# A windowed attention and token-mixing kernel in one written-out order of tasks: another order, other engines and homes for the small steps

## The chip, the cores and the metric

The kernel runs on one core of one Trainium2 chip. The metric is the device time of one execution in microseconds. The kernel before takes 250.66 us (median of three runs: 250.23, 250.66, 251.75).

## The reference

For four batches of eight heads, 768 positions and head width 64, the reference does attention in which a query sees the first four keys (sinks) and the 128 keys up to itself. The heads side by side are the rows x of a block with 512 columns. The block mixes positions and then columns:

```python
scores = np.where(is_sink | in_window, scale * (q @ k.T), -1e9)
x = softmax(scores) @ v                      # heads side by side: [4, 768, 512]
a1 = alpha1 * x + beta1
tok = np.einsum('ts,bsd->btd', w_tok, a1)    # w_tok 768 x 768
u = x + lam * tok
a2 = alpha2 * u + beta2
ch = np.maximum(a2 @ w_ch1, 0.0) @ w_ch2     # 512 -> 2048 -> 512
return u + lam * ch
```

All inputs and the output are float32 in device memory.

## The kernel before

**A list of tasks.** The kernel first builds a list of 1230 tasks, numbered in the order in which the program's loops create them. A task is one to a few dozen instructions on one engine: a load, a cast, the six transposes of one tile, the scores of one tile, one group of matmuls, one relu. Each knows the tasks it needs and the buffers it uses. Then `Plan.emit` writes the tasks out, and four tables written into the source say how:

- `ORDER` is the sequence of task numbers. Every engine executes its own instructions in this order, and never passes one that waits.
- `ENGINES` has one digit for each task: 0 is ScalarE (ACT), 1 VectorE (DVE), 2 TensorE (PE), 3 GpSimd (POOL), 4 SyncE (SP). SP only issues DMAs; ACT issues some as well and POOL issues those of w1, which are cast on the way.
- `HOMES` has one hexadecimal digit for each buffer, in the order in which tasks first use it. A buffer of a kind (say "nat") lives in one of the kind's homes (say 8), and must wait until every reader of the buffer that was there before has finished. A load into an occupied home so waits on the engine's queue that issues it, and every load behind it in that queue waits as well.
- `IDLES` puts warm-up matmuls of no use ahead of five tasks, to keep PE going at the start (67 ahead of task 46, 25 ahead of task 90).

The kinds that matter here are "nat" (8 homes, a pair of heads of q or k in float32, all 768 positions), "vnat" (4, a tile of v), "wst" (4, two 128-row blocks of w_ch2 in float32, at the start also three tiles of v), "d" (4 banks of PSUM) and "E", "x", "xh", "u16", "hT" for what lies between.

**The stages.** Batch 0 is handled first. Loads of q, k and v (tasks 6 to 25; `load_qk`, L413, `load_v0`, L441), the transposes of q and k on PE with their evacuation into qkT (`trans`, L505: cast, six transposes on L532 or L535, then the evacuation through the helper `copy`, L168 on ACT or L170 on the others), scores (L640 to L709), exponentials on ACT (L667, L714), masks (L682 on DVE, L607 on POOL), the product with v (L739, L746) with normalisation (L771, L772), halves of the scaled x (xh, L781 on POOL or DVE) and the token mix (`tok`, L868, matmuls on L880). w_tok is loaded in six tiles, scaled on ACT (L842) or DVE (L844) and transposed by PE (wT, L837). Casts of v (vfs) go through `cast_v0` (tasks 63 to 67).

Then each batch b goes through the two column matmuls while the next batch's attention is interleaved: PE alternates groups of four matmuls of h (`mlp1`, L952, matmuls L960; relu on ACT L966 or DVE L968) and of ch (`mlp2`, L1260, L1269) with the attention tasks of batch b+1. Batches 1 to 3 replace part of the two column matmuls by seven products of sums (`prod`, L1163, L1199; sums of the weights `w1S` on L993 and `w2s` on L1114), batch 3 in pairs (`mlp1_pair`, L1021, L1041). At the end the adds on L1212 and stores on L1218 write the last output.

**Loads around the change.** w_ch1 comes in four chunks of which POOL issues the requests (`load_w1`, L474, L476: tasks 32 to 35). A small DMA on SP (`gate`, L481, L483) lets SP wait for a chunk's landing before it goes on: task 36 holds the eight q and k loads of batch 1 (170 to 177; `load_qk`, L425) and those of w_ch2 (`load_w`, L469, L472) until chunk 1 has landed. w_ch2's blocks are multiplied into f16 as w2f (`cast_w2`, L854, L859; tasks 181 to 202) in pairs from one "wst" buffer. The casts of batch 1's q and k tiles are tasks 363, 366, 369, 372, 375, 378, 381 and 384, the transposes that follow each one are the numbers one higher.

Of the kernel before, what the change touches and what calls it, by code (L numbers as in the profile page):

```python
# [80 lines left out]
def kernel(  # L81
# [129 lines left out]
    for r in range(NR):  # L211
# [18 lines left out]
        6, 7, 0, 26, 1, 10, 5, 2, 9, 11, 45, 18, 8, 19, 48, 3, 22, 15, 46, 4, 49, 12,  # L230
        50, 14, 17, 47, 13, 16, 90, 43, 103, 39, 41, 91, 28, 72, 104, 95, 53, 54, 63,
        51, 42, 73, 52, 21, 44, 74, 20, 96, 109, 100, 40, 107, 110, 65, 24, 68, 108, 92,
        69, 55, 61, 56, 93, 97, 101, 98, 59, 30, 94, 102, 111, 23, 99, 62, 113, 57, 114,
        25, 112, 116, 60, 105, 115, 58, 27, 128, 64, 106, 117, 31, 131, 135, 29, 129,
        125, 132, 138, 66, 130, 179, 78, 126, 122, 178, 140, 118, 139, 123, 197, 127,
        136, 119, 137, 32, 70, 146, 120, 141, 133, 33, 84, 79, 134, 124, 144, 147, 80,
        85, 71, 150, 121, 86, 142, 75, 67, 154, 143, 151, 76, 148, 158, 155, 145, 152,
        77, 87, 166, 156, 159, 81, 162, 167, 160, 88, 163, 82, 168, 89, 213, 157, 164,
        34, 35, 83, 209, 153, 217, 149, 214, 218, 210, 229, 219, 211, 215, 212, 226,
        165, 216, 36, 230, 185, 220, 161, 177, 223, 222, 176, 232, 221, 224, 204, 225,  # L240
        175, 227, 257, 169, 237, 233, 279, 238, 199, 234, 171, 258, 273, 280, 231, 186,
        259, 228, 274, 182, 277, 172, 260, 241, 278, 174, 246, 200, 295, 170, 248, 247,
        291, 296, 37, 181, 187, 243, 293, 292, 242, 289, 198, 294, 384, 267, 188, 290,
        281, 268, 173, 271, 349, 282, 180, 285, 272, 358, 301, 351, 286, 378, 303, 189,
        203, 297, 302, 192, 304, 249, 366, 190, 379, 298, 250, 287, 369, 380, 385, 205,
        288, 283, 191, 375, 386, 367, 265, 284, 368, 352, 370, 363, 376, 266, 253, 381,
        377, 371, 299, 254, 372, 615, 364, 206, 300, 382, 201, 365, 373, 275, 374, 383,
        357, 261, 276, 183, 387, 408, 262, 614, 263, 409, 202, 269, 184, 411, 410, 395,
        264, 239, 621, 617, 412, 397, 240, 270, 388, 400, 396, 235, 616, 196, 244, 398,
        401, 255, 245, 236, 390, 256, 193, 359, 389, 251, 399, 207, 311, 195, 252, 391,  # L250
        424, 426, 393, 335, 392, 360, 425, 636, 312, 194, 427, 208, 336, 394, 648, 428,
        413, 634, 419, 414, 622, 404, 420, 337, 405, 429, 402, 415, 313, 422, 416, 421,
        361, 441, 305, 403, 442, 638, 423, 626, 406, 314, 640, 619, 437, 315, 430, 443,
        316, 435, 431, 641, 338, 436, 362, 618, 433, 306, 438, 649, 341, 317, 432, 407,
        444, 637, 644, 307, 345, 439, 339, 620, 318, 445, 434, 628, 635, 450, 642, 308,
        451, 340, 440, 452, 639, 446, 453, 417, 319, 447, 645, 323, 418, 320, 309, 448,
        643, 658, 321, 324, 623, 449, 322, 329, 625, 659, 454, 646, 325, 347, 647, 330,
        455, 343, 326, 344, 353, 355, 464, 456, 465, 348, 466, 460, 650, 457, 467, 327,
        458, 331, 629, 461, 459, 462, 653, 632, 651, 463, 656, 332, 654, 356, 472, 627,
        652, 333, 342, 310, 38, 655, 660, 624, 480, 473, 468, 469, 470, 474, 885, 665,  # L260
        471, 476, 481, 475, 482, 488, 477, 350, 483, 492, 489, 478, 630, 490, 657, 493,
        479, 514, 491, 516, 328, 515, 882, 663, 518, 880, 517, 879, 498, 666, 661, 664,
        502, 499, 354, 508, 519, 512, 346, 509, 662, 678, 513, 671, 484, 679, 676, 486,
        503, 504, 487, 485, 677, 506, 877, 672, 680, 548, 507, 526, 505, 549, 334, 674,
        631, 522, 527, 907, 546, 681, 523, 633, 903, 528, 547, 534, 878, 529, 890, 675,
# [12 lines left out]
        986, 773, 752, 913, 886, 761, 919, 774, 604, 767, 918, 598, 762, 763, 768, 777,
        764, 779, 920, 923, 780, 987, 988, 989, 990, 914, 991, 992, 993, 755, 915, 778,
        608, 756, 926, 930, 735, 609, 924, 927, 931, 925, 753, 736, 781, 737, 893, 928,  # L280
        775, 782, 738, 892, 929, 934, 754, 932, 769, 610, 935, 941, 770, 819, 776, 894,
        942, 939, 820, 821, 940, 937, 936, 823, 749, 822, 748, 945, 824, 938, 747, 827,
        933, 948, 950, 750, 943, 952, 951, 825, 953, 787, 828, 944, 807, 788, 797, 826,
        808, 949, 946, 829, 954, 798, 801, 830, 791, 802, 947, 956, 792, 783, 957, 994,
        995, 996, 997, 961, 789, 784, 962, 958, 963, 964, 955, 790, 785, 959, 811, 965,
        805, 812, 786, 795, 806, 960, 967, 796, 799, 793, 968, 970, 966, 972, 794, 813,
        969, 971, 815, 973, 814, 809, 800, 974, 816, 803, 810, 976, 804, 978, 837, 975,
        979, 977, 835, 838, 980, 841, 836, 818, 839, 843, 842, 840, 981, 845, 844, 998,
        846, 817, 1002, 832, 831, 1006, 999, 1003, 1000, 1014, 1007, 1004, 1001, 833,
# [1193 lines left out]
```

## Time and profile before

| | before |
|---|---|
| median of three runs | 250.66 us |
| span of the profiled execution | 248.4 us |
| the profiled execution's own time beside its span | not listed apart; the runs' median is 2.26 us above the span |
| PE busy | 242.9 us (98%) |
| DVE busy | 208.0 us (84%) |
| ACT busy | 136.1 us (55%) |
| POOL busy | 126.0 us (51%) |
| moved by DMA | 38.80 MB |

The profile is one execution. Its page lists the busy time of each engine, 40 slices of the span with the share of each engine and of the DMA engines in tenths, the chain of work that ended last, and the groups of instructions by source line. Other views are the timeline of one engine (start and duration in us, engine, line, operation, output and input, and in brackets the engine's idle time before it with what released it), the busy time by windows, and the answers for one tile or one line (durations in ns as min/median/max, with the first and last start). SPq, POOLq and ACTq are the queues that issue DMAs; what such a row shows as its duration is the issue, not the transfer.

### The profile page before, as it was taken

To read this page: it belongs to the slowest core of one execution; us is meant where nothing else is said; L and a number is where in the kernel's file an instruction comes from. 1 tells how busy PE (TensorE), PEld (TensorE's weight loads), DVE (VectorE), ACT (ScalarE), POOL (GpSimd) and SP (SyncE) were. 2 spreads that over 40 slices of the span, in tenths; PEclk is the share of its full clock that TensorE was granted. 3 is DMA by queue.
4 is the path that set the end of the run, shared out by engine and by line. 5 is a ranking of instruction groups with operands and counts; after the bars stand their busy time and mean duration, and the time that the engine had idled before them with its cause. 6 is when DMAs were issued, how large, how long until landed. Compare 5 with 4: busy or idle time off the path is not lost.

```text
span 248.4 us, 5583 instructions
## 1 busy us (share of the span) xinstructions
PE 242.9 (98%) x2151; PEld 159.2 (64%) x2151; DVE 208.0 (84%) x437; ACT 136.1 (55%) x229; POOL 126.0 (51%) x139
## 2 busy tenths in 40 slices
PE   8899999999999999999999999999999999999994
PEld 8654645676555544565677577568668477667883
DVE  6797987677697896798789998979798999899873
ACT  2399935688987124687833353666771234766000
POOL 8808733968866647413874012053746036556060
PEclk9999999999999999999999999999999999999999
DMA  6999999999999998899469445611000055200114
GB/s 207 210 247 297 248 211 304 355 362 287 219 196 210 254 179 178 180 247 200 106 131 203 85 84 161 170 21 45 3 0 3 4 101 186 93 0 3 65 42 150
DMA packets 86562, 38.80 MB, mean 156 GB/s; under 512 B 73588, under 2 KB 81276, under 8 KB 86536
## 3 DMA queue, kind: packets, MB, share of 16 engines
q1 hardware_dynamic: 67408, 29.11, 50.3%
q10 hardware_dynamic: 15384, 6.06, 10.4%
q0 software_dynamic: 3744, 3.28, 8.2%
q8 instruction: 17, 0.28, 0.5%
q14 instruction: 9, 0.07, 0.1%
HBM read 29.91 MB, written 6.29 MB: 146 GB/s over the span
## 4 chain that ended last, share of the span: by engine, by line
PE 90%; ACT 4%; DVE 3%; issue 2%; DVEq 0%; ACTq 0%
PE h L960 24%; PE P L1199 22%; PE tok L880 12%; PE ch L1269 8%; PE hA L1041 4%; PE pv L746 4%; PE S L645 4%; PE idle L161 2%; PE hE L1041 2%; PE tp L535 1%; ACT wt L842 1%; ACT E L667 1%; PE hB L1041 1%; DVE qkT L170 1%; PE tp L532 1%
## 5 line engine op out<-in xcount | busy, mean ns | idle before, releaser
L960 PE MATMUL h<-uT,w1f 128*128 128x384 f16 x384 | 68.0, 326 | 0.1
L960 PEld LDWEIGHTS <-w1f 128*128 128x128 f16 x384 | 35.9, 98 | 24.0 <-issue 2.0
L1199 PEld LDWEIGHTS <-hT 128*128 128x128 f16 x408 | 39.4, 98 | 6.6 <-DVE hT L1142 0.3
L667 ACT ACTIVATE E<-S 128x1024 f16<-128x1024 f32 (+1 forms) x39 | 38.0, 1002 | 7.0 <-PE S L645 5.4
L966 ACT ACTIVATE hT<-h 128x384 f16<-128x384 f32 x58 | 27.9, 492 | 21.5 <-PE h L960 17.9
L790 POOL TENSOR_TENSOR tm<-x,la_b 128x512 f32<-128x512 f32 x18 | 24.7, 1371 | 21.9 <-DVE xh L793 12.0
L880 PE MATMUL tok<-xh,wtokT 128*128 128x512 f16 x144 | 32.8, 379 | 0.0
L968 DVE TENSOR_SCALAR hT<-h 128x384 f16<-128x384 f32 x38 | 20.4, 553 | 8.1 <-PE h L960 7.7
L168 ACT CAST u<-x 128x512 f16<-128x512 f32 x17 | 10.4, 618 | 29.2 <-DVE x L887 28.0
L1199 PE MATMUL P<-w2f,hT 128*128 128x256 f16 x216 | 26.4, 273 | 0.0
L1212 DVE TENSOR_TENSOR x<-x,P 128x256 f32<-128x256 f32 x45 | 18.0, 415 | 7.2 <-PE P L1199 6.9
L880 PEld LDWEIGHTS <-wtokT 128*128 128x128 f16 x144 | 13.8, 98 | 15.2 <-issue 0.2
L1199 PE MATMUL P<-w2s,hT 128*128 128x256 f16 x192 | 22.9, 273 | 0.0
L1269 PE MATMUL ch<-w2f,hT 128*128 128x512 f16 x96 | 22.7, 379 | 0.0
L772 DVE TENSOR_TENSOR x<-pv,rec 128x256 f32<-128x256 f32 x48 | 20.4, 425 | 1.7
L168 ACT CAST n<-nat 128x768 f16<-128x768 f32 x20 | 16.2, 830 | 8.1 <-DMA out_dram<-x 4.8
L746 PEld LDWEIGHTS <-E 128*128 128x128 f16 x328 | 15.2, 97 | 4.9 <-issue 1.1
L170 POOL CAST u<-x 128x512 f16<-128x512 f32 x7 | 4.6, 663 | 26.1 <-DVE x L887 16.9
L746 PE MATMUL pv<-vfs,E 128*128 128x65 f16 x328 | 17.7, 194 | 0.0
L887 DVE TENSOR_TENSOR x<-x,tok 128x512 f32<-128x512 f32 x24 | 15.9, 681 | 1.8 <-PE tok L880 1.5
L607 POOL TENSOR_SCALAR_AFFINE_SELECT E<-E 128x512 f16<-128x512 f16 x12 | 8.6, 740 | 16.9 <-ACT E L667 16.9
L170 POOL CAST vfs<-vnat 128x512 f16<-128x512 f32 x18 | 13.9, 778 | 5.1 <-PE pv L746 4.2
(161 smaller groups left out, 432.4 us busy)
## 6 DMA issues: line engine op xcount, KB each, us to landing
wst_w<-in_moe_w_ch_dram SPq DMA_DIRECT2D x8, 512.0 KB, 7.9
nat<-in_q_dram SPq DMA_DIRECT2D x10, 384.0 KB, 4.2
nat<-in_k_dram SPq DMA_DIRECT2D x10, 384.0 KB, 8.2
vnat<-in_v_dram SPq DMA_DIRECT2D x14, 256.0 KB, 6.2
out_dram<-x SPq DMA_DIRECT2D x11, 256.0 KB, 3.3
wtn<-in_moe_w_tok_dram SPq DMA_DIRECT2D x6, 384.0 KB, 4.4
w1f<-in_moe_w_ch_dram POOLq DMA_DIRECT2D x4, 512.0 KB, 10.6
out_dram<-x ACTq DMA_DIRECT2D x7, 256.0 KB, 4.5
```

Source lines behind the costliest of these rows:

```text
L168: nc.scalar.copy(o, i)
L170: engine[e].tensor_copy(o, i)
L667: nc.scalar.activation(eT.t, pS.t[:, :, 0 : n * w].rearrange("p e (i w) -> p e i w", i=n), AF.Exp, scale=scale)
L746: nc.tensor.matmul(po.t[:, hl, :], eT.t[:, e_, off + i, c : c + P], vf[j][:, h, :], start=(r < 2 and n == 0), stop=(n == len(parts) - 1 an ...
L772: nc.vector.tensor_mul(bx.t[:, 4 * G : 4 * G + 4, :], po.t[:, :, 0:D], rec.t.to_broadcast([P, 4, D]))
L790: engine[e].tensor_mul(bt.t, bx.t.rearrange("p h d -> p (h d)"), la1_b)
L880: nc.tensor.matmul(bank(), wtokT[:, si, ti * P : (ti + 1) * P], hs[si].t, start=(si == 0), stop=(si == NR - 1))
L960: nc.tensor.matmul(ph.t, w1f[:, c, fi * P : (fi + 1) * P], bu.t[:, c, chk * NTOK : (chk + 1) * NTOK], start=(c == 0), stop=(c == NC - 1))
L966: nc.scalar.activation(bh.t[:, fi, :], ph.t, AF.Relu)
L968: nc.vector.tensor_scalar_max(bh.t[:, fi, :], ph.t, 0.0)
L1199: nc.tensor.matmul(pc.t, hh[:, nt * P : (nt + 1) * P], w(fi), start=(first and n_ == 0), stop=(n_ == HF - 1), skip_group_check=True)
L1269: nc.tensor.matmul(pc.t, bh.t[:, fi, nt * P : (nt + 1) * P], w2f[:, fi, :], start=(fi == 0), stop=(fi == NF - 1))
```

## The change

Only the strings `ORDER`, `ENGINES` and `HOMES` change; tasks, their instructions and `IDLES` are the same. The head of the order before and after:

```diff
     ORDER = (
-        6, 7, 0, 26, 1, 10, 5, 2, 9, 11, 45, 18, 8, 19, 48, 3, 22, 15, 46, 4, 49, 12,
-        50, 14, 17, 47, 13, 16, 90, 43, 103, 39, 41, 91, 28, 72, 104, 95, 53, 54, 63,
...
+        41, 42, 6, 45, 0, 46, 47, 7, 48, 49, 50, 90, 91, 26, 72, 10, 9, 11, 18, 95, 8, 96,
+        1, 2, 53, 51, 52, 19, 5, 103, 104, 54, 109, 110, 22, 107, 108, 15, 12, 14, 100, 101,
...
     HOMES = (
-        "145602340010102001213310200221013302203140101100511203013044215120821000003331a501103130"
...
+        "05270473602100210101022310103023330233305014010111130012213000b5005211a13184104302112100"
...
     )
```

What the strings say, worked out by task:

- **Counts by engine** (tasks, before and after): ACT 243 and 236, DVE 367 and 365, PE 383 and 383, POOL 122 and 138, SP 115 and 108.
- **Start.** The evacuation 47 (q of the first tile) moves from DVE to ACT; the products 41 and 42 (the spread of beta) come first on DVE. The casts of v 66 and 67 move from DVE to POOL; five halves of xh move from POOL to DVE. POOL's order from there is 115, 66, 118, 67, 127, 121, 124, 32, 33, 34, 156, 35, 168; before, 32 and 33 came after 127, and 34 and 35 last.
- **Requests on SP.** The order is the same up to task 203. Then it was 192, 205, 191, 615, 206, 614; it is 205, 614, 191, 615, 619, 206. Request 192 (wst_w2_10) goes to ACT's queue behind 387.
- **Homes of loads.** nat1_2_1 (175) goes into the home of nat1_3_1 (177, cast by 384), nat1_2_0 (174) into that of nat1_0_1 (171, cast by 366); both went into homes whose readers were long done. wst_w2_8 (191) goes into the home whose second reader is 189.
- **Casts of batch 1.** 363, 366, 369, 378 and 384 move from ACT to POOL, in the order 384, 366, 358 (a cast of v), 378, 369, then the products 188 and 190, then 375, 363, 381, 372. Five evacuations of transposes move from DVE to ACT.
- **w2f.** 182, 187, 189, 194, 195 and 200 move from POOL to DVE. On DVE 193 and 194 come ahead of the masks 412, 401, 399 and the products 196 and 195.
- **Later.** 18 relus move from DVE to ACT and 25 from ACT to DVE; 11 casts of u from ACT to POOL and six back; five masks from POOL to DVE and six from DVE to POOL; seven sums w1S from DVE to POOL; ten output stores from SP to ACT and five back.
- **PE.** The groups stand in a slightly different order: before the first transpose of batch 1, for one, group 249 of h now follows instead of preceding it. Runs of whole-array and half-array matmuls alternate 66 times instead of 70.

More of the change, by code (lines that the diff above doesn't have):

```diff
@@ L321 @@
-        "4404404404433333304040404043404040202010121203012121312010121213320103212131203012121312"
-        "0321213321213111111111111111112104210421040011210421342134010111332021202201120211202120"
-        "2211320211202121220132121320202022013202112021212201120213202020220112021320202122013202"
-        "11202020220132021111112020210202142141111212121212121211302133021314210214210214210214"
+        "3313134433443333444444444444444433334443111211201212021212020203333321211210200210201210"
+        "2020201202011202020202020213213213213213211202002020202020211121112131211121112131444444"
@@ new lines @@
+        "4444411114413134011114411314444442213221321321120021021321020202020120210202020202021212"
+        "1202021212020202121202120212021202121212122221022221422221022221422221422221033311111311"
+        "3133133333332032132032132032032032002020101212010121213120101212131201012121312010121213"
+        "1203212131212131213421042134111121342104210410002121202020212021212121202121202120202020"
+        "2021202111212021202120212111212021202121111121212121212121332131211121021421021021021044"
@@ new lines @@
+        "4444004040443333333404040434040404120201012120303212133203032121312010121213120101212133"
+        "2032121312121312134213421040000210421042134100021212120212120202020202021212020212120202"
+        "0212120112120202121202020112020212121211111212121212121211321332131210210214214214210000"
+        "4444040004033333304340434040404041202010121201032121312030121213320101212133203012121332"
+        "0321213321213331111113333113312104213421040000213421042104011011132120202201321211202020"
@@ L325 @@
+        "2211120211202020221112021320212022011202112120202201120211202021220132021321202022011202"
+        "11202020220132121111112020210202102141111212121212121213302113421310214214214210210214"
     )
     HOMES = (
-        "145602340010102001213310200221013302203140101100511203013044215120821000003331a501103130"
-        "5140011112031102051467032311003221123033120133001001032002203212113003320023113113103113"
-        "20311022642130030020210001112300123101450093004101001b3002014531200000131101000502017200"
@@ new lines @@
+        "5031201300121001014504626033002213223322113300021033112133003101132003230323112123101213"
+        "303210216142200301012322301020001502014230201041013311000001420063103100300920020500b200"
+        "5217310110031320302102121331301332233310001232135012230123230211210110326730601232230000"
+        "23120101030125004100501131002000100345150040112121800301000300101a3102320010302233110301"
+        "0011202220111102223215712300123320031203311320030770752120111022020010421012006200001501"
@@ L335 @@
+        "0221050112311b00201034509004110001101117300301230001321023001031210123100221322003321351"
+        "32000233421502311203030110257321000013"
     )
```

15 lines of the change are left out of this document (removed), and 150 rows, old and new, of the table ORDER.

## The prediction

> **What bounds the kernel now.** I read the page first: the busy line, the slices and the chain.
>
> ```profile
> span 248.4 us, 5583 instructions
> PE 242.9 (98%) x2151; PEld 159.2 (64%) x2151; DVE 208.0 (84%) x437; ACT 136.1 (55%) x229; POOL 126.0 (51%) x139
> ...
> DMA  6999999999999998899469445611000055200114
> ...
> PE 90%; ACT 4%; DVE 3%; issue 2%; DVEq 0%; ACTq 0%
> ```
>
> PE is busy for 242.9 of 248.4 us and is 90% of the chain. The change keeps every task, so PE's own work stays; an order can only win what PE loses between its instructions. The DMA row is at nine tenths or more for the first third: there, a load lands when the backlog lets it. Next, the windows by stage (busy time and, in brackets, instructions of each engine; then the granted clock, DMA share and GB/s).
>
> ```profile
> core 0: us, PE busy (x) PEld busy (x) DVE busy (x) ACT busy (x) POOL busy (x), PEclk, DMA share, GB/s
> ...
> 39.00:49.00 10.00, 9.94 (x69) 6.14 (x68) 7.54 (x14) 5.67 (x11) 7.63 (x7) 1.00 1.10 347
> 49.00:60.00 11.00, 11.00 (x105) 7.54 (x103) 7.55 (x12) 10.07 (x19) 8.21 (x9) 1.00 1.09 338
> ...
> 204.00:228.00 24.00, 24.00 (x167) 16.09 (x165) 22.78 (x51) 14.88 (x34) 15.11 (x11) 1.00 0.24 77
> ```
>
> The clock is 1.00 in each. From 49 us PE has no gap at all; its idle time lies in the first 40 us and at the end. So I go through the start for the gain, and through each later stage only for new waits. The last microseconds first:
>
> ```profile
> 243.74 1.47 PE L1199 MATMUL P<-w2f,hT 128*128 128x256 f16 x12
> ```
> ```profile
> 245.25 0.42 DVE L1212 TENSOR_TENSOR x<-x,P 128x256 f32<-128x256 f32 x1 [0.38 <-PE P L1199]
> ```
>
> The last matmul ends at 245.2, one add follows, and the store's landing ends the span at 248.4. This end keeps its shape. The median of three runs is 250.66, so 2.26 us lie outside the profiled span; I add them back unchanged.
>
> **Part 1, the start: −0.4.** These are the waits that the new order touches.
>
> ```profile
> 7.68 1.82 DVE L170 COPY qkT<-tp 128x768 f16<-128x768 f16 x2 [1.59 <-PE tp L535]
> ```
> ```profile
> 9.55 0.29 PE L709 MATMUL S<-qkT 64*128 64x256 f16 x2 [0.52 <-DVE qkT L170]
> ...
> 12.35 0.27 PE L161 MATMUL idle<-warm 128*128 128x128 f16 x2 [0.30 <-DVE qkT L170]
> ...
> 29.96 0.51 PE L837 MATMUL wT<-iden,wt 128*128 128x128 f16 x6 [0.24 <-ACT wt L842]
> ```
>
> DVE evacuates the first two transposes one after the other, 1.82 us, and the first scores wait for both. The new ENGINES gives one (task 47) to ACT, idle then, so both end near 8.7 and the scores start about 0.7 earlier. The two later waits, 0.30 and 0.24, go partly as well: up to −0.9. Against it stands POOL.
>
> ```profile
> 22.33 1.57 POOL L476 DMA_DIRECT2D w1f<-in_moe_w_ch_dram  x2
> 23.90 2.13 POOL L781 TENSOR_TENSOR xh<-x,la_b 128x256 f16<-128x256 f32 x3
> ...
> 31.65 1.55 POOL L476 DMA_DIRECT2D w1f<-in_moe_w_ch_dram  x2
> ```
> ```profile
> 26.02 0.95 DVE L170 CAST vfs<-v 128x768 f16<-128x768 f32 x1
> ```
>
> The new order puts the two casts of v's last tiles (66, 67) on POOL, ahead of three token-mix halves (127, 121, 124), the first w1f requests (32, 33) and then 34, 156, 35 and 168. Task 67 needs a load that DVE, busy until then, found landed at 26.0; POOL would come to it near 22, where its first w1f requests stand now. I take a landing half-way, 24.0. Then come one cast of 0.83 (row below), three halves of 0.71, three requests of 0.78 and half 156: done near 30.0, where the token mix now starts behind the 29.96 row, at 30.3. So POOL caps the gain: I take −0.4, with ends of −0.9 (landing by 22) and +1.7 (at 26.0). The first w1f requests start some 5 us later but all four are out before 33.2, the end of the last row, and with DMA full their last landing changes little: nothing.
>
> **Part 2, the q/k loads of batch 1: +2.1 and +0.4.** The new HOMES puts nat1_2_1 (task 175) into the home of nat1_3_1 (177) and nat1_2_0 (174) into that of nat1_0_1 (171). In the old strings 175 has a free home:
>
> ```profile
> 38.06 0.40 SPq L425 DMA_DIRECT2D nat<-in_k_dram  x1
> ...
> 39.58 2.84 SPq L425 DMA_DIRECT2D nat<-in_k_dram  x2
> ```
>
> These are 177's request, then 175 and 171. In the new order SP stops at 175 until 384, the cast of nat1_3_1, has read the home; 171, 186, 172, 174, 170, 198, 173 and 180 stand behind it on SP's queue. The casts 384, 366, 378 and 369 also move from ACT to POOL.
>
> Landing times come from the page's DMA issues (the last column is the median in us) and from the view of the tile nat.
>
> ```profile
> nat<-in_q_dram SPq DMA_DIRECT2D x10, 384.0 KB, 4.2
> nat<-in_k_dram SPq DMA_DIRECT2D x10, 384.0 KB, 8.2
> ```
> ```profile
> DMA to landing us min/median/max: 3.1/5.7/9.3
> ```
> ```profile
> 49.34 0.61 POOL L170 CAST vfs<-vnat 128x512 f16<-128x512 f32 x1
> 50.47 2.50 POOL L859 TENSOR_TENSOR w2f<-wst_w,lam_b 128x512 f16<-128x512 f32 x2 [0.53 <-DMA wst_w<-in_moe_w_ch_dram]
> 53.02 0.82 POOL L170 CAST n<-nat 128x768 f16<-128x768 f32 x1
> ```
>
> 177, issued at 38.06 into the backlog, lands after 5.7 (median of all) to 8.2 (median of k); I take 6.6, hence 44.7. Cast 384: 45.5. Then 175 goes out, 5.9 us later than now, and 171 at 46.0. By then SP has asked for nothing for six microseconds and the backlog is short, so I take the lower median, 4.2: 171 lands at 50.2. POOL runs 366, 358, 378 in that order: 50.2 + 0.83 + 0.61 + 0.83 = 52.5. At the ends (5.7 and 3.1; 8.2 and 5.7) it is 50.5 and 55.6. Who waits: the transpose tp1_2_1 (379).
>
> ```profile
> 48.71 2.93 PE L960 MATMUL h<-uT,w1f 128*128 128x384 f16 x17
> 51.47 0.50 PE L535 MATMUL tp<-iden,n 128*128 128x128 f16 x6
> 51.80 0.81 PE L960 MATMUL h<-uT,w1f 128*128 128x384 f16 x4
> 52.45 0.50 PE L535 MATMUL tp<-iden,n 128*128 128x128 f16 x6
> ...
> 57.46 1.46 PE L960 MATMUL h<-uT,w1f 128*128 128x384 f16 x8
> 58.86 0.61 PE L645 MATMUL S<-qkT 64*128 64x256 f16 x8
> ```
>
> In PE's new queue one group of four h matmuls (249) less stands ahead of it; such a group takes 52.45 − 51.80 = 0.65, so it is reached at 51.47 − 0.65 = 50.8, with the gain of part 1 at 50.4. The stall is 52.5 − 50.4 = 2.1 (0.1 to 5.2). All of PE is behind it in order, so nothing covers it. The loads do not wait for PE, so what part 1 gains or loses before this point only lengthens or shortens this stall: 52.5 − 50.8 = +1.7 stands as long as the stall does.
>
> The second place: 174 waits for cast 366 (51.05), lands at 55.3; POOL does 369 and two w2f products (188, 190, 2.50 together) until 55.9, then the casts 375, 363, 381, 372 at 0.83: 59.2. The last transpose, tp1_1_1, starts at 57.1 now (57.46 less its 0.33) and would stand at 58.8 after the net +1.7: +0.4.
>
> **Part 3, fewer tiling changes: −0.4.** Eight h matmuls from 57.46 to the scores at 58.86 take 1.40, twice 0.65 would be 1.30: 0.1 for a change between whole-array and half-array matmuls. Counting runs along PE's queue, 70 become 66.
>
> **Part 4, w2: 0.** wst_w2_8 (191) now waits on SP for cast 189, moved from POOL to DVE behind the last q/k copy; wst_w2_10 (192) moves to ACT's queue behind the ks copy; six casts move from POOL to DVE.
>
> ```profile
> wst_w<-in_moe_w_ch_dram SPq DMA_DIRECT2D x8, 512.0 KB, 7.9
> ```
> ```profile
> L859 DVE TENSOR_TENSOR w2f<-wst_w,lam_b x7: 681/684/1221, 41.1 to 63.9; 128x512 f16<-128x512 f32 x7
> ```
> ```profile
> 67.45 0.69 DVE L682 TENSOR_TENSOR E<-E,mask 128x1024 f16<-128x1024 f16 x1 [1.60 <-ACT E L667]
> ```
>
> The last transpose at 59.2 takes 0.33, its copy 0.95 and 189 0.68: 191 goes out near 61.2, and lands at 65.4 (4.2, the emptier queue) to 69.1 (7.9). DVE then runs 193, 194, three masks and 196, 195 in order, each 0.68 or 0.69: seven times is 4.8, ending at 70.2 to 73.9. Their first reader (313) stands about half a microsecond before the old place of 337, the third group of the row below:
>
> ```profile
> 67.38 2.75 PE L1269 MATMUL ch<-w2f,hT 128*128 128x512 f16 x12
> 69.97 0.41 PE L746 MATMUL pv<-vfs,E 128*128 128x65 f16 x8
> 70.31 0.61 PE L645 MATMUL S<-qkT 64*128 64x256 f16 x8
> ```
>
> The scores end near 70.9, so with +1.7 PE comes to 313 near 72.6. Without the backlog it is covered with 2.4 to spare; with it, 1.3 of stall. I take 0, bounds 0 and 1.3. The Trainium skill, "DMA: Bandwidth & Descriptors", section "Queues, rings and completion order", says that each DMA engine takes packets from its queue rows in turn; by that, wst_w2_10 on ACT's own row would pass SP's backlog and the end at 73.9 would be pessimistic. Without that rule the sum is +1.7 to +3.0, with it +1.7.
>
> **Part 5, the later swaps: 0.** Between 204 and 228 DVE has 24.00 − 22.78 = 1.22 us free. Counting the swaps there, DVE gets in net about one and a half pieces of the size of a relu (first row below, ns), 0.75 us: it fits, with 0.5 left. Elsewhere swaps go both ways. Seven w1S sums move from DVE to POOL, whose nearest row is the second:
>
> ```profile
> L968 DVE TENSOR_SCALAR hT<-h x38: 542/554/559, 41.7 to 182.0; 128x384 f16<-128x384 f32 x38
> ```
> ```profile
> L1114 POOL TENSOR_TENSOR w2s<-w2f x2: 1152/1242/1333, 48.2 to 88.6; 128x512 f16<-128x512 f16 x2
> ```
>
> At 1.24 each they are 8.7 us of POOL, and their readers in the queues come tens of microseconds later. The Trainium skill's "GPSIMD Engine Reference", section "Specifications", speaks against this: POOL shares SBUF interfaces with DVE and contends with two-input DVE work. The 1221 against 684 ns of DVE's w2f product would fit it, but one such stretch is 0.5 us on an engine that PE does not wait for. Batch 2's transposing loads also change places; I find no term for them, up to +1.
>
> Sum: −0.4 + 2.1 + 0.4 − 0.4 = **+1.7**, span 250.1, time 250.66 + 1.7 = **252.3**. A measurement of this kernel tells about 1%, 2.5 us, from no change.
>
> **Rivals.** (a) *The loads are covered.* If 177 lands after 5.7 or less and 171 after 3.1, cast 378 is done at 50.5 and part 2 costs 0.1 and nothing. Left are −0.4 to −0.9 and −0.4: about −1.0, **249.7**. For: ACT is busy 10.07 of 11 us from 49 to 60 and POOL 8.21, so POOL may even be the better place for the casts. Against: the DMA share of 1.10 from 39 to 49, which makes the low landing unlikely for 177.
> (b) *The backlog holds w2 as well.* Late w2 rows block DVE in order, with masks and normalisations queued behind, so that PE's attention work stops too: part 4 at 1.3, and the upper half of part 2 adds about one more: +1.7 + 1.3 + 1 = +4.0, **254.7**. It decides once 191 needs over 6.6 to land. For: 7.9 is the median of its row. Against: SP's six silent microseconds thin the queue.
> (c) *DVE becomes the bound from 204 on*, because the added 0.75 us meets a stage with 1.22 free: +0.75 on top of the sum, **253.1**. For: the busiest DVE stage; against: 0.5 us stay free.
> That the change does nothing is excluded: it moves requests and homes; at worst its effects cancel.
>
> **How the numbers follow.** Forecast 0.50, (a) 0.22, (b) 0.18, (c) 0.10. Faster by over 1% means below 248.2: it needs more than PE's whole recoverable time, 0.04. Slower by over 1% means above 253.2: most of (b), half of (c) and the upper end of the forecast, 0.28. The rest, 0.68, is within. The range goes from the lower side of (a), 249.4, to (b), 254.8; the forecast alone, 251.0 to 253.3.
>
> **What would show it.** Right: SP idle before the second nat request after 38 us, waiting for POOL's cast, and PE idle before L535 near 50 with POOL's n as releaser; the first scores near 8.9; POOL's w1f requests after 27. Wrong: no PE idle from 42 to 60 (then (a)), or PE idle in 68 to 75 behind DVE's w2f (then (b)); a time under 250 refutes part 2.

## The result and the profile after

The kernel after takes 268.52 us (median of four runs, 267.79 to 270.02) against 250.66 us: the ratio is 1.070, with an interval of 1.066 to 1.075. It is 17.9 us slower; the forecast was 1.7. One timed execution below, 270.87 us in run 3, is 1.65% above the other of its kernel, counts as slow and is not compared. The page of after, in the order in which the page of before was read:

```profile
span 266.6 us, 5573 instructions
...
PE 247.0 (93%) x2151; PEld 160.5 (60%) x2151; DVE 204.8 (77%) x437; ACT 128.5 (48%) x213; POOL 138.9 (52%) x156
...
PE   8299999999999897769979999899999999999995
...
PEclk9869999999999999999999999999999999999999
...
PE 53%; DMA 19%; DVE 7%; issue 7%; SPq 6%; POOL 6%; ACT 1%; DVEq 0%; POOLq 0%; ACTq 0%
```

The span is 18.2 us longer, and PE's share falls from 98% to 93%. The chain that ended last was 90% PE; now 19% of it is DMA and 6% SP's queue. The PE row shows the two places: the second slice (7 to 13 us) and the slices 16 to 18 (100 to 120 us). The clock row has an 8 and a 6 at the start where before has only nines.

The windows by stage, first of before (rows that the prediction did not need), then of after:

```profile
0.00:10.00 10.00, 8.29 (x108) 7.92 (x109) 6.43 (x24) 1.41 (x2) 9.25 (x23) 1.00 0.91 209
10.00:20.00 10.00, 9.66 (x148) 5.36 (x149) 9.38 (x23) 8.62 (x16) 2.93 (x4) 1.00 1.17 237
95.00:140.00 45.00, 45.00 (x398) 29.22 (x397) 37.77 (x78) 27.46 (x44) 22.96 (x24) 1.00 0.85 168
```
```profile
0.00:10.00 10.00, 5.39 (x67) 5.22 (x67) 2.90 (x17) 1.28 (x1) 6.53 (x18) 1.00 0.86 192
10.00:20.00 10.00, 8.21 (x81) 5.92 (x82) 5.30 (x13) 3.62 (x6) 2.21 (x4) 0.66 1.09 223
...
95.00:140.00 45.00, 38.01 (x278) 19.91 (x276) 30.54 (x65) 21.83 (x33) 25.86 (x30) 1.00 0.80 153
204.00:228.00 24.00, 24.00 (x191) 17.41 (x189) 19.78 (x39) 7.55 (x13) 14.18 (x12) 1.00 0.26 65
```

PE's loss is in the first 20 us (4.35 us less busy work than before, some of it at a low clock) and between 95 and 140 us, where before had no gap and after has 7.0 us of them. From 204 on it has none.

To place the loss, each PE task of a changed kernel is set beside the point at which the kernel before has done as much PE work; the difference of the two start times is PE's delay there. Worked out so from the traces:

| time in before, us | 6 | 12 | 36 | 48 | 60 | 78 | 84 | 96 | 102 | 108 | 120 | 126 | 150 | 156 | end |
|---|---|---|---|---|---|---|---|---|---|---|---|---|---|---|---|
| delay of after, us | 4.7 | 6.8 | 6.7 | 6.8 | 7.6 | 7.8 | 8.9 | 8.6 | 14.3 | 15.0 | 16.5 | 17.0 | 17.0 | 18.2 | 18.1 |

The profile is one execution, and the point of equal work is not sharp where tasks changed places, so a few tenths of a microsecond say nothing. 6.8 us are lost at the start, about 6 when the scores of batch 2 begin, and the rest in pieces of about one. Nothing is lost after 156.

**The start.** Before, then after, each the timelines of DVE and PE; in after, ACT's request for the row as well:

```profile
3.96 0.71 DVE L170 CAST n<-nat 128x768 f16<-128x768 f32 x1 [0.23 <-DMA nat<-in_q_dram]
...
9.42 1.14 DVE L1319 TENSOR_TENSOR lb_b<-lb_b,lam_r 128x512 f32<-128x512 f32 x1
```
```profile
6.81 0.83 PE L535 MATMUL tp<-iden,n 128*128 128x128 f16 x12
7.48 1.56 PE L161 MATMUL idle<-warm 128*128 128x128 f16 x25
```
```profile
3.57 0.50 ACTq L205 DMA_DIRECT2D lb_b<-in_moe_beta_dram  x1
```
```profile
9.60 0.69 DVE L1315 TENSOR_TENSOR lb_b<-lb_b,lam_r 128x512 f32<-128x512 f32 x1 [6.01 <-DMA lb_b<-in_moe_beta_dram]
...
10.94 1.01 DVE L170 CAST n<-nat 128x768 f16<-128x768 f32 x2
```
```profile
11.54 1.46 PE L531 MATMUL tp<-iden,n 128*128 128x128 f16 x12 [5.11 <-DVE n L170]
13.25 2.83 PE L161 MATMUL idle<-warm 128*128 128x128 f16 x25 [0.25 <-ACT qkT L168]
16.01 0.61 PE L705 MATMUL S<-qkT 64*128 64x256 f16 x4
```

The product 41 now stands first on DVE. It reads a small row that ACT asks for at 3.57 and that is there at 9.60. DVE takes its instructions in order, so the first casts of q and k, which before start at 3.96 and 4.97 as their loads land, go out at 10.94, and the transposes at 11.54 instead of 6.81. PE is idle for 5.1 us; after that the same 25 warm-up matmuls take 2.83 instead of 1.56 us.

**Batch 1.** Timelines of SP, POOL and PE of after:

```profile
49.64 1.68 SPq L421 DMA_DIRECT2D nat<-in_k_dram  x2
```
```profile
55.25 0.83 POOL L170 CAST n<-nat 128x768 f16<-128x768 f32 x1 [5.63 <-DMA nat<-in_k_dram]
...
56.58 0.83 POOL L170 CAST n<-nat 128x768 f16<-128x768 f32 x1
```
```profile
57.74 0.83 PE L531 MATMUL tp<-iden,n 128*128 128x128 f16 x12
...
64.73 0.51 PE L531 MATMUL tp<-iden,n 128*128 128x128 f16 x6 [0.58 <-POOL n L170]
```

SP's stop at 175 is there: the request goes out at 49.64, right behind cast 384 (POOL 48.51 to 49.61), against 39.58 before. But cast 378 is done at 57.41 and PE, 6.8 us late already, comes to its transpose at 57.74 without a wait: the stall is hidden behind the loss at the start, as run 1 shows.

**Batch 2.** SP and PE of before, then SP, POOL and PE of after:

```profile
76.63 11.29 SPq L551 DMA_TRANSPOSE qkT<-n  x7
```
```profile
95.18 0.67 PE L645 MATMUL S<-qkT 64*128 64x256 f16 x8
```
```profile
69.78 10.46 SPq L431 DMA_DIRECT2D vnat<-in_v_dram  x4
...
102.17 3.41 SPq L547 DMA_TRANSPOSE qkT<-n  x2
```
```profile
77.64 0.68 POOL L170 CAST vfs<-vnat 128x512 f16<-128x512 f32 x1 [7.51 <-DMA vnat<-in_v_dram]
```
```profile
106.63 0.29 PE L641 MATMUL S<-qkT 64*128 64x256 f16 x2 [1.45 <-DMA qkT<-n]
108.52 0.39 PE L641 MATMUL S<-qkT 64*128 64x256 f16 x4 [1.60 <-DMA qkT<-n]
...
115.79 2.11 PE L956 MATMUL h<-uT,w1f 128*128 128x384 f16 x12 [1.91 <-DVE uT L902]
```

Four requests for v tiles keep SP from 69.78 to 80.24. They share two homes in the new order; request 207 waits until POOL, which waits for the landing of 206, has cast it (77.64), and stands on SP from 73.7 to 78.3. What follows on SP is late with it: the loads for batch 2 and then the eight transposing loads that make its qkT. Before had seven of them out by 87.9 and the eighth by 91.4; after issues the last from 104.3 on, and the first scores of batch 2 wait for them (1.45 and 1.60 us). The transposing loads of u stand behind them on SP (from 105.67), and PE waits another 1.91 us for uT.

### The profile page after: what moved, and what is told of

Its sections match the earlier page's. It is cut to its first block, busy times and chain, and to the rows that moved or that the text cites. A ratio compares the mean times of both kernels' runs of the same rounds, so it can differ in the third digit from the quotient of the medians.

```text
span 266.6 us, 5573 instructions
## 1 busy us (share of the span) xinstructions
PE 247.0 (93%) x2151; PEld 160.5 (60%) x2151; DVE 204.8 (77%) x437; ACT 128.5 (48%) x213; POOL 138.9 (52%) x156
## 4 chain that ended last, share of the span: by engine, by line
PE 53%; DMA 19%; DVE 7%; issue 7%; SPq 6%; POOL 6%; ACT 1%; DVEq 0%; POOLq 0%; ACTq 0%
PE P L1195 18%; PE h L956 10%; PE tok L876 6%; DMA nat<-in_k_dram 5%; DMA vnat<-in_v_dram 4%; PE hA L1037 4%; SPq L547 3%; DMA qkT<-n 3%; PE pv L742 3%; DMA nat<-in_q_dram 2%; DMA lb_b<-in_moe_beta_dram 2%; DMA uT<-u 2%; PE hE L1037 2%; PE S L641 2%; PE S L636 1%
## 5 line engine op out<-in xcount | busy, mean ns | idle before, releaser
L956 PE MATMUL h<-uT,w1f 128*128 128x384 f16 x384 | 69.4, 326 | 3.6 <-DVE uT L902 2.2
L962 ACT ACTIVATE hT<-h 128x384 f16<-128x384 f32 x51 | 24.6, 493 | 27.5 <-PE h L956 27.3
L876 PE MATMUL tok<-xh,wtokT 128*128 128x512 f16 x144 | 34.0, 379 | 0.0
L964 DVE TENSOR_SCALAR hT<-h 128x384 f16<-128x384 f32 x45 | 24.3, 553 | 8.6 <-PE h L956 8.0
L786 POOL TENSOR_TENSOR tm<-x,la_b 128x512 f32<-128x512 f32 x18 | 25.8, 1432 | 9.4 <-DVE xh L789 6.5
L1208 DVE TENSOR_TENSOR x<-x,P 128x256 f32<-128x256 f32 x45 | 18.1, 418 | 9.9 <-PE P L1195 8.8
L170 POOL CAST vfs<-vnat 128x512 f16<-128x512 f32 x18 | 12.3, 689 | 16.4 <-DMA vnat<-in_v_dram 16.4
L170 POOL CAST u<-x 128x512 f16<-128x512 f32 x12 | 9.0, 752 | 22.6 <-DVE x L883 21.4
L168 ACT CAST u<-x 128x512 f16<-128x512 f32 x12 | 7.3, 617 | 27.0 <-DVE x L883 26.9
L170 POOL CAST n<-nat 128x768 f16<-128x768 f32 x12 | 10.4, 880 | 14.2 <-DMA nat<-in_k_dram 9.2
L641 PE MATMUL S<-qkT 64*128 64x256 f16 (+1 forms) x156 | 12.8, 269 | 3.1 <-DMA qkT<-n 3.1
```

Of the source, the lines that this page charges most:

```text
L170: engine[e].tensor_copy(o, i)
L641: nc.tensor.matmul(pv_[:, e_, i, :], o.t[rows, 2 * hp + 1, j * P : (j + 1) * P], o.t[rows, 2 * hp, j * P : j * P + w], start=not bias, sto ...
L786: engine[e].tensor_mul(bt.t, bx.t.rearrange("p h d -> p (h d)"), la1_b)
L876: nc.tensor.matmul(bank(), wtokT[:, si, ti * P : (ti + 1) * P], hs[si].t, start=(si == 0), stop=(si == NR - 1))
L956: nc.tensor.matmul(ph.t, w1f[:, c, fi * P : (fi + 1) * P], bu.t[:, c, chk * NTOK : (chk + 1) * NTOK], start=(c == 0), stop=(c == NC - 1))
L962: nc.scalar.activation(bh.t[:, fi, :], ph.t, AF.Relu)
```

## The experiments

Each of the twelve kernels was run beside the kernel before on the same chip. The theory after the result: three waits at the heads of in-order queues make the loss, each for a load: DVE's for beta's row, SP's for the q/k homes, SP's for the v homes and the order of batch 2's requests. The rivals are named with each run.

**1. Beta's products later** (`e1_beta_later`): after, with 41 and 42 behind 54.

```diff
-        41, 42, 6, 45, 0, 46, 47, 7, 48, ..., 104, 54, 109, 110,
+        6, 45, 0, 46, 47, 7, 48, ..., 104, 54, 41, 42, 109, 110,
```

> The changed kernel with tasks 41 and 42 (the product and shuffle of beta) moved from the front of the order to behind 54, so that DVE meets them after the first four evacuations. Theory A: of the 18 us, 6.8 come from DVE standing 6.0 us at task 41 for an 8 KB load while the casts of the first q and k tiles wait behind it (4.7 us), and from TensorE's clock going down meanwhile (some 2 us). Then the first scores come near 9.8 in place of 16.0, the granted clock is 1.00 from 10 to 20, and the span falls from 266.6 to about 260; if the stall that the prediction saw at the first transposes of batch 1 was only covered by the late start, it comes up now and the span is 261 to 262. Rival B: the loads set the time, the late start is hidden behind them anyway: the span stays above 265.

264.86 us (263.64 to 266.08), 1.055 of before (1.034 to 1.076); the profiled span is 261.8, 4.8 less than after's. PE's timeline, and POOL's:

```profile
9.18 0.39 PE L704 MATMUL S<-qkT 64*128 64x256 f16 x4
...
10.96 0.53 PE L527 MATMUL tp<-iden,n 128*64 128x128 f16 x12 [0.78 <-DMA n<-in_q_dram]
...
53.88 0.84 PE L530 MATMUL tp<-iden,n 128*128 128x128 f16 x12 [1.22 <-POOL n L170]
...
62.43 0.51 PE L530 MATMUL tp<-iden,n 128*128 128x128 f16 x6 [1.39 <-POOL n L170]
```
```profile
23.72 0.83 POOL L170 CAST vfs<-v 128x768 f16<-128x768 f32 x1 [0.36 <-DMA v<-in_v_dram]
...
51.67 0.83 POOL L170 CAST n<-nat 128x768 f16<-128x768 f32 x1 [4.83 <-DMA nat<-in_k_dram]
```

The scores start at 9.18 instead of 16.01, and the clock is 1.00 from 10 to 20 us. Of the 6.8 us only 4.8 come back in the end: PE's delay is 0.25 us at 12, 1.5 at 48 (three waits for small transposes whose loads are not there, the first is the second row), but 5.3 at 60. The stall at the q/k transposes of batch 1 has come up, 3.8 us, since PE is now early enough to meet it.

**2. The same move in the kernel before** (`e2_beta_first`).

```diff
-        6, 7, 0, 26, 1, 10, ..., 43, 103, 39, 41, 91, ..., 51, 42, 73,
+        41, 42, 6, 7, 0, 26, 1, 10, ..., 43, 103, 39, 91, ..., 51, 73,
```

> The kernel before with one thing changed: tasks 41 and 42 go to the front of the order, ahead of the casts 45 and 48 on DVE. Theory A: the first transposes start near 11.5 in place of 6.8, the clock falls between 10 and 20 and the span grows by 5 to 7 us, to about 254 to 255.5. Rival B: the later stages have slack and take most of it back: the span grows by less than 2 us. Rival C: it needs the other moves of the start as well: below 3 us.

254.84 us, 3.7 more than before in the median, 1.015 of it (1.008 to 1.022); span 253.2, 4.8 more. DVE, then PE:

```profile
8.26 0.69 DVE L1314 TENSOR_TENSOR lb_b<-lb_b,lam_r 128x512 f32<-128x512 f32 x1 [4.68 <-DMA lb_b<-in_moe_beta_dram]
```
```profile
10.48 1.29 PE L530 MATMUL tp<-iden,n 128*128 128x128 f16 x12 [4.09 <-DVE n L170]
11.56 2.87 PE L161 MATMUL idle<-warm 128*128 128x128 f16 x25
```

The one move costs 3.7 us at the first transposes and 4.8 at the scores, and the kernel before absorbs none of it later: the delay is 4.8 from 12 us to the end. This shows the cause at the start by itself. The row came 4.7 us after its request here and 6.0 in after; that may be why after's runs spread, which is not shown.

**3. Warm-ups that bridge the wait** (`e3_more_idle`): after, with 134 instead of 67 warm-ups ahead of task 46. This parts the wait from the low clock behind it.

```diff
-        (46, 0, 67),
+        (46, 0, 134),
```

> The changed kernel with 134 warm-up matmuls in place of 67 ahead of the first transposes, so that TensorE is kept busy while DVE waits. Theory A (part of the loss is the clock): the granted clock stays at 1.00 from 10 to 20, where it was 0.66, the first scores come near 14 in place of 16, and the span falls by about 2 us, to 264.5. Rival: the clock costs nothing because evacuations bound that stretch: the span stays within 0.5 of 266.6.

266.47 us in one execution (after: 267.79 to 270.02); its profiled span is 264.5. PE:

```profile
11.95 0.98 PE L530 MATMUL tp<-iden,n 128*128 128x128 f16 x12 [1.83 <-DVE n L170]
13.34 1.55 PE L161 MATMUL idle<-warm 128*128 128x128 f16 x25 [0.42 <-ACT qkT L168]
14.83 0.39 PE L704 MATMUL S<-qkT 64*128 64x256 f16 x4
```

The row came later still (DVE 41 at 10.00), so the transposes are 0.4 later than in after, yet the scores are 1.2 earlier: the 25 warm-ups take 1.55. The delay at 12 us is 5.1 against 6.8. So with an even longer wait the delay is 1.7 us smaller: that is the low clock. After's own 6.8 are 4.7 at the first transposes and 2.0 behind them. One timed execution is too little to show this in the time by itself.

**4. Two requests of batch 2 alone** (`e4_batch2_loads`): after, with load 617 (a k tile of batch 2) moved ahead of the first transposing request 637 on SP, and ACT's cast 909 (batch 3) behind cast 638 (batch 2).

```diff
-        ..., 428, 208, 337, ..., 306, 318, 617, 436, ..., 453, 448, 909, 879, 449, 638,
+        ..., 428, 208, 617, 337, ..., 306, 318, 436, ..., 453, 448, 879, 449, 638, 909,
```

> The changed kernel with two moves: the request of nat2_1_1 (617) goes on SP's queue from behind the output store 316 and the transposing load 637 to right behind 208, and ACT's cast 909 (of batch 3) from ahead of cast 638 (of batch 2) to behind it. Theory A: the 6 us that TensorE loses from 96 to 108 on the old kernel's time scale come from the transposed tiles of batch 2 that arrive last behind these two waits; the span falls from 266.6 by 3 to 6 us, to 261 to 263.5, and the idle time before the first scores of batch 2 goes. Rival: other homes or SP's row of transposing loads at 1.3 us each hold the last tile anyway: less than 1 us.

268.25 us, 1.069 of before (1.062 to 1.075); span 266.1, 0.5 less than after, with 0.3 more lost at the start. The transposing requests begin at 88.8, no earlier than in after (87.15): SP comes to them late, whatever their order. The forecast of 3 to 6 us fails. What the edit does at the scores themselves this run can't show: PE reaches them at 108.64, as late as after's last wait for qkT ends (108.52), and so waits for none. DVE waits 3.08 us for an output store at 93.30, and PE 1.93 and 0.71 us behind DVE; it still waits 2.41 us for uT at 116.63.

**5. The q/k homes** (`e5_q_k_homes`): run 1 with nat1_2_1 in home 7 and nat1_2_0 in home 3, whose readers are long done.

```diff
-...1001014504626033002213223322...
+...1001014503726033002213223322...
```

> The kernel of e1 (beta's two tasks later) with two digits of HOMES changed: nat1_2_1 goes to home 7 and nat1_2_0 to home 3, whose readers are long done, so that SP does not wait for the casts 384 and 366. Theory A (the prediction's part 2, uncovered by e1): e1 loses 3.8 us between 48 and 60 on the old time scale at the transposes of batch 1; that goes, and with it part of what batch 2 loses, since SP's whole queue runs some 5 us earlier: the span falls from 261.8 to 255 to 258. Rival B: the queue of the DMA engines is full there, so the loads land no earlier: the span stays above 261. Rival C: POOL's row of casts is what is late, not the loads: the span falls by 1 us at most.

261.22 us (260.04 to 262.40), 1.041 of before (1.036 to 1.045); span 260.4. SP, then PE:

```profile
40.26 3.54 SPq L420 DMA_DIRECT2D nat<-in_k_dram  x2
```
```profile
52.47 0.84 PE L530 MATMUL tp<-iden,n 128*128 128x128 f16 x12
...
100.95 0.28 PE L640 MATMUL S<-qkT 64*128 64x256 f16 x2 [1.81 <-DMA qkT<-n]
```

Request 175 goes out at 40.26, PE has no idle time at the transposes, and the delay at 60 us falls from 5.3 to 1.9. So the homes make the stall, 3.4 of its 3.8 us. The end gains only 1.4 us in the span (3.6 in the median, whose two runs differ by 2.4). At batch 2's scores, which still wait for transposing loads, the delay is 2.7 smaller than in run 1 (8.5 against 11.2 at 102). Most of the rest goes between 108 and 126, where the delay grows from 9.1 to 10.6 as PE waits for DVE (0.90 us for x, 0.38 for hT), while it stays at 12.2 in run 1. 255 to 258 was too hopeful.

**6. The v homes** (`e6_q_k_v_homes`): run 5 with vnat1_2 in home 1 and vnat1_3 in home 0.

```diff
-...3503726033002213223322...
+...3503726033002213210322...
```

> e5 with two more digits of HOMES: vnat1_2 goes to home 1 and vnat1_3 to home 0 of the four homes of v tiles, where the new string uses homes 2 and 3 alone, so that vnat1_3, vnat1_4 and vnat1_5 do not wait in SP's queue for a cast on POOL that waits for the load ahead. Theory A: SP's wait of 4.9 us ahead of vnat1_4 goes, batch 2's loads and transposing loads come that much earlier, and the loss of some 6 us at the first scores of batch 2 goes: a span 3 to 6 us below e5's. Rival: batch 2's own homes and order (617 behind 644, ACT's 909 ahead of 638) hold it: less than 1.5 us.

259.43 us, 1.033 of before (1.030 to 1.037); span 258.4, 2.0 less than in run 5. PE:

```profile
99.67 0.39 PE L640 MATMUL S<-qkT 64*128 64x256 f16 x4 [0.47 <-DMA qkT<-n]
```

The delay at 102 us falls from 8.5 to 5.5: the v homes are part of batch 2's loss. 1.7 of these 3.0 us are the clock: the twelve token-mix matmuls behind the scores take 4.45 us at a granted clock of 0.50 in run 5 (in run 1 as well) and 2.76 here. Part of it is no gain, since PE then waits 2.02 us for uT here and 0.50 in run 5. The 2.0 us of span lie between the theory (3 to 6) and the rival (under 1.5), and the timed executions of runs 5 and 6 overlap. SP still stands, for the homes of w2's rows and of a later v tile.

**7. Both, and the two requests of run 4** (`e7_homes_and_loads`): run 6 with the edit of run 4.

```diff
-        ..., 428, 208, 337, ..., 306, 318, 617, 436, ..., 453, 448, 909, 879, 449, 638,
+        ..., 428, 208, 617, 337, ..., 306, 318, 436, ..., 453, 448, 879, 449, 638, 909,
```

> e6 with the two moves of e4 as well (617 behind 208, 909 behind 638). Alone these two gave 0.5 us. Theory A (several waits in a row, the v homes ahead of them): now that SP comes to them earlier, they give 1 to 3 us over e6, and the span comes to 250 to 252. Rival: they stay without effect: within 0.7 us of e6.

258.48 us, 1.030 of before (1.026 to 1.033); span 255.7, 2.7 less than in run 6. PE:

```profile
98.12 0.72 PE L640 MATMUL S<-qkT 64*128 64x256 f16 x8
...
105.82 2.11 PE L955 MATMUL h<-uT,w1f 128*128 128x384 f16 x12 [2.01 <-DVE uT L901]
```

The scores of batch 2 run without a stall; in run 6 the wait was 0.47. That the edit is worth 2.7 us here is not shown. 0.9 of them are there at 48 us (delay 1.0 against 1.9), before its requests go out; 0.3 come at batch 2's scores, and 1.5 at 150 to 156, where run 6 waits 1.32 us for batch 3's qkT. In the medians the gain is 0.95, and the executions of the two runs overlap. The time of 250 to 252 that was expected is missed by over 6. What is left over before is 7.3 us of span: about 1.1 up to 54 us, 1.0 at 78 to 84, 3.5 at 96 to 108 (the row above: batch 2's qkT requests stand ahead of the transposing loads of u on SP), 0.7 up to 126 and 1.0 at 150 to 156. These pieces are placed, not tested.

**8. Only task 47, in the kernel before** (`e8_before_47_act`): the one edit that part 1 counted as a gain.

```diff
 ENGINES, the digit of task 47
-1
+0
```

> The kernel before with one digit of ENGINES changed: evacuation 47 goes from DVE to ACT, the one move of the start from which the prediction hoped for 0.7 us. If that was right the first scores start near 8.9 in place of 9.55 and the span falls by 0.3 to 0.7 us, time about 250.2. Rival: ACT's copy is followed by nothing that gains, because the next evacuations and ACT's exponentials bound the stretch to the token mix: within 0.2 us.

250.73 us in 11 runs against 251.02 in 15 of before: 0.9984 (0.9973 to 0.9995). ACT, DVE and PE:

```profile
8.42 0.80 ACT L168 COPY qkT<-tp 128x768 f16<-128x768 f16 x1 [3.03 <-PE tp L530]
```
```profile
8.76 0.96 DVE L170 COPY qkT<-tp 128x768 f16<-128x768 f16 x1 [2.75 <-PE tp L530]
```
```profile
8.56 1.56 PE L161 MATMUL idle<-warm 128*128 128x128 f16 x25
10.05 0.28 PE L704 MATMUL S<-qkT 64*128 64x256 f16 x2
```

The two evacuations run side by side, and the scores follow the warm-ups without a wait. From the first transposes to the scores it takes 2.16 us (7.89 to 10.05) against 2.74 in before. The scores still start later than before's 9.55, and not near 8.9, because the 67 warm-ups ahead take 6.70 us in this execution and 5.62 in before's. It is the one version here that beats both kernels, by 0.16% (0.05 to 0.27%), 0.3 us in the medians.

**9. The same with fewer warm-ups** (`e9_47_act_18_idle`), since they now end last ahead of the scores.

```diff
-        (90, 1, 25),
+        (90, 1, 18),
```

> e8 with 18 warm-up matmuls in place of 25 ahead of the first scores. In e8 the two evacuations end at 9.22 and 9.72 and the first scores start at 10.05, behind the last warm-up matmul: the warm-up has become the bound. Theory: the scores start about 0.3 us earlier against the first transposes and the time falls by 0.2 to 0.4 us, to 0.9965 to 0.9975 of before. Rival: the stretch behind is bound by ACT and DVE, which take it back: the same as e8, 0.998 to 0.999.

250.84 us in 12 runs against 250.88 in 17: 1.0001 (0.9988 to 1.0015). Nothing is gained over before, and neither the theory nor its rival had that; why the gain of run 8 is gone as well is open.

**10. The old engines under the new order** (`e10_old_engines_late`): run 7, with the old engine for the 113 tasks from 456 on that are no DMAs and had changed theirs.

> e7 (span 255.7, 7.3 us above before) with the old engines for the 113 tasks from batch 1's token mix on whose engine the change swaps and that are no DMAs; order and homes stay. The prediction gave these swaps 0. If the swaps are what is left, the span falls by 2 us or more, to below 253.7; if what is left is order and homes, it stays within 1.5 us of 255.7, and may be longer, since the new order was written for the new engines.

296.14 us (one run), span 294.0, 38 us more than run 7. PE's delay grows from 10 us at 108 to 45 at 234, as PE waits in many places for swapped work (5.0 us in all for ACT's uT ahead of L955, 3.5 for DVE's E ahead of L741); the mean granted clock is 0.965.

Taken together, the later swaps are no cost to the new order: without them it is far worse. Order and engines belong together, and this run can't price a swap by itself.

**11. The old queues for the later DMAs** (`e11_old_dma_queues`): run 7, with the old issuing engine for the 27 requests from 209 on that had changed theirs.

> e7 with the old issuing engine for the 27 DMA requests (loads from batch 2 on, output stores) that the change moves between SP and ACT. If requests on ACT's queue hold ACT's casts and exponentials up (or SP's late requests are what is left), the span falls by 1 us or more from 255.7; the rival is no effect, within 0.7 us, or a loss, because SP's queue, already the one that is late for batch 2, gets ten more.

266.59 us (one run), span 264.5, 8.8 more than run 7. PE waits 2.5 us at 135 for a cast of v, 1.8 at 139 behind it and 2.3 at 167 for qkT.

Giving requests back to SP makes what stands behind them late, v tiles and qkT by these waits. The move of stores and loads from SP to ACT is worth something to the new order.

**12. The small rows first** (`e12_rows_first`): after, with the memsets and the requests for the rows of beta and lambda ahead of ACT's other requests. This asks whether the row is late because it is asked for late.

```diff
-    nc.scalar.dma_start(ab_row[0:NC], moe_alpha2.rearrange("(c p) -> c p", p=P))
...
+    for o_ in (lb1_b, lam_r, la1_b):
+        nc.vector.memset(o_, 0.0)
+
+    for o_, src in ((lb1_b, moe_beta1), (lam_r, moe_lam), (la1_b, moe_alpha1)):
+        nc.scalar.dma_start(
+            o_.rearrange("(a i) d -> a i d", i=32)[:, 0, :], src.unsqueeze(0).to_broadcast([4, DM]))
+    nc.scalar.dma_start(ab_row[0:NC], moe_alpha2.rearrange("(c p) -> c p", p=P))
```

> The changed kernel (tasks 41 and 42 still first on DVE) with the small requests of ACT's queue in another order: beta's row, lam's row and alpha's row ahead of the two of ab_row, and their memsets first on DVE, so that the two rows that task 41 needs are asked for near 1.4 and 2.0 us in place of 3.6 and 2.3. What sets the 6.0 us that DVE waits for 8 KB? Theory A, the loads of q, k and v that SP and POOL ask for from 0.8 us on stand ahead and clear late, whenever the small request comes: DVE still gets to task 41 at 9 to 10 us, the span stays within 1 us of 266.6. Rival B, a fixed time per request: 41 starts near 8.0, span 264.5 to 265.5. Rival C, early enough it passes the backlog: 41 starts before 6.5, and the start's loss goes: span below 262.5.

264.57 us, 1.053 of before (1.044 to 1.062); span 263.7, 2.9 less than after. DVE:

```profile
8.67 0.69 DVE L1315 TENSOR_TENSOR lb_b<-lb_b,lam_r 128x512 f32<-128x512 f32 x1 [5.08 <-DMA lam_r<-in_moe_lam_dram]
```

Lambda's row, asked for at 2.72, is there at 8.67, again 6.0 us after its request; beta's row, asked for at 1.56, was there by then. The later of the two requests that 41 needs goes out 0.85 earlier than in after, and 41 starts 0.93 earlier. So the wait looks like a time per request, of about 6 us, and not like a fixed backlog that ends at 9.6; one run of each can't exclude chance, since the times spread from 4.7 to 7.1. Task 41 at 8.67 and the span lie between theory A and rival B. Of the span's 2.9 us only 0.9 come from the start; the rest lies between 108 and 126, where after loses 2.0 us and this run none.

## Why the prediction was wrong, point by point

The steps that bring after back to before add up, in spans of one execution each: 4.8 us for beta's place (run 1), 1.4 for the q/k homes (5), 2.0 for the v homes (6), 2.7 for batch 2's requests (7) and 7.3 not undone, together 18.2. In the medians of the timed runs they are 3.7, 3.6, 1.8, 0.95 and 7.8. The first two steps are clear of the spread of the runs; the third and the fourth are not, and rest on the waits in their traces. The steps are in this order and not independent.

- **Part 1, the start, −0.4: this step failed.** It priced task 47 and the casts 66 and 67, but 41 and 42, "first on DVE" in the list of the change, were given no term; they cost 6.8 us at the start of after and 4.8 in run 2, where they move alone. The question that part 2 asks of SP's queue (what is at its head, and what does that wait for) was not asked of DVE's. The rows to answer it were there: before runs 41 at 9.42 without a wait, behind casts that start at 3.96, and nothing reads its result before 30 us. The sign "scores near 8.9" failed at 16.01; in run 1 it is 9.18. Of the prices that were given, that of 47 was too high: the scores were to start 0.7 earlier, but the row at 9.55 has an idle time of 0.52, and the 25 warm-ups ahead of it end at 9.04. Run 8 measures 0.3 us in the medians. The casts were right: cast 67 came to its load at 23.7 in run 1 (forecast 24.0), and the w1f requests went out from 26.8 to 31.1. Even without 41 and 42 the start is no gain: in run 1 PE is 1.4 us late at 36, not 0.4 early, as it waits for loads of n that part 1 does not name. That this lies under the upper end of +1.7 is luck; that end stood for a late cast 67.
- **The clock: no term.** The granted clock falls to 0.50 behind PE's idle time, which costs 1.7 (run 3) to 2.0 us (from the first transposes to 12 us in after). By windows of one microsecond it is low from 11.0 to 17.8 in after, from 10.9 to 14.3 in run 2, from 10.2 to 17.0 in run 12, and nowhere from 7 to 18 in run 3, where PE was idle for 1.83 us. One window of after and one of run 2:

```profile
16.00:17.00 1.00, 1.00 (x15) 0.58 (x16) 0.00 (x0) 0.55 (x2) 0.00 (x0) 0.50 0.89 248
```
```profile
15.00:16.00 1.00, 1.00 (x22) 0.65 (x22) 0.00 (x0) 0.89 (x2) 0.03 (x1) 1.00 1.22 265
```

The Trainium skill, "TensorE: Matmul & The Clock Gate", section "Part 1: The HAM clock gate (the "warmup" mystery)", says that the clock is halved after an idle window of some 3.4 us and given back after a busy one of about the same length. The halving agrees with the trace, though 2.96 us of idle time were enough in run 12. The return agrees in run 2, where PE is at work all through the low stretch of 3.4 us. In after and run 12 the stretch is 6.8 us, twice as long; there PE comes back 0.5 us after the clock has fallen and pauses once for 0.25. So the same move costs 2.0 us behind the wait in after and 1.1 in run 2.
- **Part 2, the q/k homes, 2.1 and 0.4: right in kind, too small, and hidden in after.** 177 took 6.4 us from its request to its cast in after (6.6 forecast), 171 took 5.1 (4.2 forecast). In run 1, 171 lands at 51.67 where 50.2 was forecast, and the two places cost PE 1.22 and 1.39 in the rows and 3.8 us in all. Run 5 takes 3.4 of it away with two digits of HOMES. The rule that was written into part 2, that loads do not wait for PE and an earlier loss only shortens this stall, is what happened in after: 0.8 us of delay is added between 48 and 60. The recorded sign of rival (a), no idle time of PE from 42 to 60, is nearly met in after (0.29 us, behind DVE's uT, none behind these casts). Yet run 1 shows that the loads are not covered; PE is only late. The second wait (0.58 at 64.73) was there. In run 1 the first place costs less than forecast (1.22, not 2.1) and the second more (1.39, not 0.4).
- **Part 3, −0.4:** no run can tell it from the rest. In the order of the traces' matmuls the changes between whole-array and half-array are 70 before and 68 after, not 66, so by its own price the term would be −0.2.
- **Part 4, w2, 0:** right. The delay grows by 0.3 us at most between 60 and 72 us in any of the runs. So rival (b) falls, and no run here decides the rule on queue rows.
- **Part 5, the later swaps, 0:** right for the swaps from 204 on. DVE is busy for 19.78 of 24 us and PE has no gap, so rival (c) falls. **Wrong for batch 2's transposing loads**, "no term, up to +1": about 6 us in after. The step looked at the loads' own place in the order and not at what stands ahead of them on SP, where v tiles in shared homes hold the queue for 4.6 us. Run 6 lowers the delay at 102 by 3.0 with two digits of HOMES, 1.7 of it through the clock; what makes the rest is not shown. It is the mechanism of part 2 once more, 25 us further on, and part 2's own method would have found the v homes: for each request on SP, the reader that must leave its home, and when.
- **Rival (a)** fell with part 2 (run 1). Every mechanism of the forecast and its rivals lay within 5 us; the range had no room for one that was not listed.

Not settled: the 7.3 us that run 7 leaves over before, of which 3.5 lie around PE's wait for the first u transposes and the rest in pieces of one; how much the requests of runs 4 and 7 are worth; and why the row takes 4.7 us in one run and 7.1 in another.

## What to carry to other kernels

When an order changes, go through every engine's queue, not only the one with the DMAs: for each instruction that moved towards the head, look up when its operand lands, and charge its wait to all that stands behind it. A load into a shared home carries the previous reader's time into an in-order request queue, and from there into loads that have nothing to do with it. A stall that the profile does not show may only be hidden behind an earlier one, so undoing one cause can give less than its size (4.8 of 6.8 us in run 1). And a step that is smaller than the spread of the runs is read from its waits, not from two spans.

## What the runs showed of the hardware

- A small row took 4.7 (run 2), 6.0 (after), 6.4 (run 3) and 7.1 us (run 4) from the start of its request to the instruction that waits for it, beside q, k and v loads that kept the DMA engines 0.86 busy over the first 10 us of after. In run 12, lambda's row took 6.0. The medians of the 384 KB loads in after are 5.7 (q) and 4.5 (k): the row, one line of 512 numbers, was not faster than they are.
- Behind an idle stretch of 3.0 to 5.3 us PE did the same 25 matmuls in 2.49 to 2.87 us (after, runs 2, 4 and 12) instead of 1.55 to 1.56.
- The low clock at the start lasted 3.4 us in run 2 and 6.8 us in after, run 4 and run 12.
- One lost interval at the start reached the end of the profiled execution in full: 4.8 us at 12 us and 4.8 at the end (run 2).
